# Attention beside a feed-forward chain: TensorE's order fixed in the first chunk, and the other chunks recorded as one spaced sequence

## The chip, the core and the metric

The kernel runs on one core of a Trainium2 chip. The metric is device time in microseconds (us), and lower is better. The engines are named as in the profile: PE is the matmul engine (PEld its weight loads, which overlap the matmuls), DVE the vector engine, ACT the scalar engine, POOL the GpSimd engine, and SP the engine whose queue issues the DMAs.

## What is computed

Attention with a hash mask, and then two feed-forward layers over its output. There are 2 batches, 8 heads, 768 positions and 64 features per head; the feed-forward layers are 512 wide with 2048 hidden features.

```python
q_bits = (np.einsum('bhsd,dk->bhsk', q, proj) > 0)          # 6 bits; the same for k
mask = q_bucket[:, :, :, None] == k_bucket[:, :, None, :]   # same 6 bits
scores = np.where(mask, scale * q @ k.T, -1e9)
scores = scores - np.max(scores, axis=-1, keepdims=True)
attn = np.exp(scores)
attn = attn / (np.sum(attn, axis=-1, keepdims=True) + 1e-09)
x = attn @ v                                                # 1536 tokens x 512
x = np.maximum(x @ w_in, 0.0) ** 2 @ w_out                  # layer 0
h = x @ w_in2
out = (np.maximum(h, 0.0) + alpha * np.minimum(h, 0.0)) @ w_out2   # layer 1
```

## The kernel before

The 1536 tokens are cut into 4 chunks of 384 (half a batch each). Attention of a chunk works on 4 pairs of heads (`Pair`). A pair has 6 score tiles (2 heads x 3 blocks of 128 queries). For each of them `scores` issues 4 matmuls of 128x384 on PE into one `s` tile, DVE takes the row maximum (`low`, line 389), ACT the exponential with its sums (`sm`, line 392), and `p_t` then turns the tile with 6 transposes on PE (line 407), three to an `m` tile, which DVE or ACT copies to `pt`. When a pair's six tiles are turned, `recip` makes the reciprocal of the sums (a small transpose into `rin`, line 437, and a trip through memory to spread it), `av` issues the 12 products with the values (line 423; the trace has 24 records for them), and `finish` scales the result and splits it into `xh` and `xl`. Before a pair's scores its queries, and in chunks 0 and 2 its keys, have to be prepared (`prepare`: hash bits, line 235; codes, line 251; splits and copies).

A feed-forward layer runs over a chunk in 16 units, one for each 128 hidden features. A unit is 12 matmuls in `hidden` (lines 613 to 615) and 9 in `project` (lines 641, 642, 645) into the tile `acc`; the projection of a unit is recorded one unit late. Layer 0 of chunk 0 starts when attention of chunk 0 has ended, and attention of chunks 1, 2 and 3 is recorded beside layer 0 of chunks 0, 1 and 2: `Background` holds a list of attention steps, and at 80 points of a chunk (`step()`) it runs as many of them as a straight line through its marks says. In the same place weights are changed from 64-bit floats to 32 bits (`to_f32`, three DVE operations and one ACT each).

The `s` tiles come from `s_tile`: in the first chunk two of them alternate, but beside the feed-forward chain there is only one, since `acc` then belongs to `project`. Codes of the keys use it too. `m` tiles rotate over three buffers in the first chunk and over two later.

What PE does next is not the recorded order alone: a scheduler goes through the recorded instructions by priority (recorded earlier is higher) and takes a later one where its own model of time says that the earlier one is not ready. `keep_in_program_order` and `issue_after` bind it. Every engine then runs its list strictly in that order, so where an instruction has to wait on the chip, all behind it on that engine wait as well.

Attention of one chunk is recorded by `attention(c, lag)`, which begins with the preparation of its first pair and ends by turning, multiplying and finishing its last one:

```python
    steps, marks = [], [(0.0, 0)]
    for c in range(1, NCH):
        steps += attention(c, 1)
        marks.append((c - 1 + LEAD, len(steps)))
    following = Background(steps, marks)
```

Of the kernel before, what the change touches and what calls it, by code (L numbers as in the profile page):

```python
# [1 line left out]

# [20 lines left out]

EVICT = ("aavaav", "avavav", "vvavva", "vvavva")

LEAD = 0.8


@with_exitstack
def kernel(  # L30
# [20 lines left out]
    nc = tc.nc  # L51
# [3 lines left out]
    P = 128  # L55
    T = S // 2
    NTB = T // P
    NKB = S // P
    NPAIR = H // 2
    NCH = NT // T  # L60
# [35 lines left out]
    def s_tile():  # L96

        state["s"] += 1
        if not state["moe"] and state["s"] % 2 == 0:
            return ps_a.tile([P, 3, 512], F32, tag="acc", name="acc")  # L100
        return ps_s.tile([P, 2, 512], F32, tag="s", name="s")

    def m_tile():

        state["m"] += 1
        if not state["moe"] and state["m"] % 3 == 0:
            return ps_h.tile([P, 512], F32, tag="h", name="h")
        return ps_m.tile([P, 512], F32, tag="m", name="m")
# [8 lines left out]
    def f32(ap):  # L117
        return ap.bitcast(F32)
# [4 lines left out]
    ident = const.tile([P, P], F32, name="ident")  # L123
# [47 lines left out]
    raw = {}  # L171
    keys = {}
    keyed = {}
    scored = {}

    def load_pair(c, j):

        b, s0 = c // 2, (c % 2) * T
        h0 = 2 * j
        kr = None  # L180
        if c % 2 == 0:
            kr = p2.tile([P, 2, S], F32, tag="kr", name="kr")
            nc.sync.dma_start(out=kr[:, 1], in_=kT[b, h0:h0 + 2].rearrange("h d s -> (h d) s"))
            if c == 0 and j == 0:
                nc.sync.dma_start(
                    out=proj_sb, in_=proj[:, 0:P].rearrange("p (h n) -> p h n", h=2)[:, :, 0:GR // 2]
                )
        qn = p2.tile([P, T], F32, tag="qn", name="qn")
        nc.sync.dma_start(out=qn, in_=qT[b, h0:h0 + 2, :, s0:s0 + T].rearrange("h d s -> (h d) s"))
        if c % 2 == 0:  # L190
            keys[b, j] = [kr, None, None]
            if c == 0 and j == 0:
                load_values(b, j)
                nc.sync.dma_start(out=ident, in_=eye)
                nc.sync.dma_start(out=alpha_sb, in_=alpha)
        raw[c, j] = qn

    def load_values(b, j):
        vr = p4.tile([P, NKB, 2 * D], F32, tag="vr", name="vr")
        keys[b, j][-1] = vr  # L200
        return nc.sync.dma_start(out=vr, in_=v[b, j])

    class Pair:
# [174 lines left out]
        def scores(self, h, t):  # L378
            ps = s_tile()
            qs = slice(t * P, (t + 1) * P)  # L380
            for a in range(2):
                ks = slice(a * HALF, (a + 1) * HALF)
                for i in range(2):
                    nc.tensor.matmul(  # L384
                        ps[:, a, 0:HALF], self.q[:, h, i, qs], self.k[:, h, i, ks], start=i == 0, stop=i == 1
                    )

            low = p4.tile([P, 1], F32, tag="low", name="low")
            low_ins = nc.vector.tensor_reduce(low, ps[:, 0:2, 0:HALF], AX.XY, ALU.max, negate=True)  # L389
            sm = sm3.tile([P, S], F32, tag="sm", name="sm")  # L390
            i = h * NTB + t
            sm_ins = nc.scalar.activation(  # L392
                sm.rearrange("p (a n) -> p a n", a=2), ps[:, 0:2, 0:HALF], AF.Exp, bias=low,
                accum_out=self.sums[:, i:i + 1],
            )
            scored[self.c, self.j, i] = (low_ins, sm_ins)
            self.p[h, t] = sm

        def p_t(self, h, t, a):
            if t == 0 and a == 0:  # L400
                self.pt[h] = p2.tile([P, NTB, NKB, P], F32, tag="pt", name="pt")
            pp = self.p[h, t]
            ps = m_tile()
            n = NKB // 2
            for i in range(n):
                b = a * n + i
                nc.tensor.transpose(ps[:, i * P:(i + 1) * P], pp[:, b * P:(b + 1) * P], ident)  # L407
            src = ps[:, 0:n * P].rearrange("p (b n) -> p b n", b=n)
            dst = self.pt[h][:, t, a * n:(a + 1) * n, :]
            if EVICT[self.c][2 * t + a] == "a":  # L410
                nc.scalar.activation(dst, src, AF.Copy)
            else:
                nc.vector.tensor_copy(dst, src)

        def av(self, part):

            if part == 0:
                self.o = m_tile()
            n = NKB // 3
            for b in range(part * n, (part + 1) * n):  # L420
                for h in range(2):
                    r = slice(h * D, (h + 1) * D)
                    nc.tensor.matmul(  # L423
                        self.o[r, 0:T], self.vr[:, b, r], self.pt[h][:, :, b, :],
                        start=(b == 0), stop=(b == NKB - 1),
                    )
            if part == 2:
                self.u = p1.tile([P, T], F32, tag="u", name="u")
                nc.scalar.activation(self.u, self.o[:, 0:T], AF.Copy)
# [17 lines left out]
        def finish(self):  # L447
            xh, xl = xT.get(self.c) or new_x(self.c)
            x = self.u
            nc.vector.tensor_tensor(x, x, self.rb, ALU.mult)  # L450
            nc.scalar.activation(xh[:, self.j, :], x, AF.Copy)
            nc.gpsimd.tensor_tensor(xl[:, self.j, :], x, f32(xh[:, self.j, :]), ALU.subtract)  # L452

    def new_x(key):
        xT[key] = (
            m2.tile([P, KDM, T], F32R, tag="xh", name="xh"),
            m2.tile([P, KDM, T], F32R, tag="xl", name="xl"),
        )
        return xT[key]

    def attention(c, lag):

        def begin():
            if (c, 0) not in raw:
                load_pair(c, 0)

        pairs = [Pair(c, j) for j in range(NPAIR)]
        steps = [begin] + pairs[0].prepare()
        late = []
        ended = []  # L470

        def tail():
            pr, h, t = late.pop(0)
            for a in range(2):
                steps.append(lambda a=a: pr.p_t(h, t, a))
            if t == NTB - 1 and h == 1:
                steps.append(pr.recip)
                for part in range(3):
                    steps.append(lambda part=part: pr.av(part))
                ended.append(pr)  # L480

        for j, pr in enumerate(pairs):
            nxt = pairs[j + 1].prepare() if j + 1 < NPAIR else []
            for u in range(2 * NTB):
                h, t = divmod(u, NTB)
                steps.append(lambda pr=pr, h=h, t=t: pr.scores(h, t))
                late.append((pr, h, t))
                for _ in range(2 if c == 0 else 1):
                    if nxt:
                        steps.append(nxt.pop(0))  # L490
                if ended and u == 3:
                    steps.append(ended.pop().finish)
                if len(late) > lag:
                    tail()
        while late:
            tail()
        while ended:
            steps.append(ended.pop(0).finish)
        return steps


    class Background:
# [52 lines left out]
    def keep(u):  # L555

        kept[u] = state["res"].tile([P, DM], F32, name="w%d_%d_%d" % u)
        nc.sync.dma_start(out=kept[u], in_=w_d[u])
# [169 lines left out]
    for step in attention(0, 2):  # L728
        step()
# [10 lines left out]
    state["moe"] = True  # L740


    steps, marks = [], [(0.0, 0)]
    for c in range(1, NCH):
        steps += attention(c, 1)
        marks.append((c - 1 + LEAD, len(steps)))
    following = Background(steps, marks)
    steps = []
    for f in range(KFF):
        for o in range(2):  # L750
# [19 lines left out]
    steps = [lambda f=f, o=o: keep((1, f, o)) for f in range(KFF) for o in range(2)]  # L770
    conversion = Background(steps, [(0.25, 0), (1.3, len(steps))])
    for n in range(NCH + 1):
        steps = second_x(n) if n < NCH else []
# [76 lines left out]
```

## Time and profile before

| | |
|---|---|
| median of 3 runs | 845.5 us (843.67 to 845.7) |
| the profiled execution's own time | 845.31 us |
| its span, from the first to the last instruction | 843.5 us |
| PE busy | 800.3 us, 95% of the span |
| PEld, DVE, ACT, POOL busy | 77%, 60%, 56%, 43% |
| mean granted clock of PE | 0.994 |

Busy shares are means over stages that differ: attention of chunk 0 alone (to about 82 us), layer 0 of chunks 0, 1 and 2 with attention beside it (to about 493 us), and then feed-forward alone. Matmuls overlap in the records, so a busy PE can still be issuing at less than its pace.

### The profile page before, as it was taken

What the parts mean: (1) busy time and instruction counts of PE and PEld (TensorE: products, weight loads), DVE (VectorE), ACT (ScalarE), POOL (GpSimd) and SP (SyncE); (2) the same over time, 40 slices, a digit from 0 to 9 for tenths busy, and PEclk for the clock granted to TensorE, in tenths of its full rate; (3) what the DMA queues carried; (4) which work ended last, traced back from release to release, by engine and by line L of the source; (5) the groups of instructions that cost most, each with busy time, mean ns of one, the idle gap of its engine ahead of it and who ended that gap; (6) DMA issues with size and microseconds to landing.
All of it is one profiled execution on the core that took longest, in us unless ns stands there. A gap on an engine that the chain in (4) does not pass through costs nothing.

```text
span 843.5 us, 12642 instructions
## 1 busy us (share of the span) xinstructions
PE 800.3 (95%) x4384; PEld 649.7 (77%) x4384; DVE 507.3 (60%) x822; ACT 473.7 (56%) x926; POOL 363.9 (43%) x321
## 2 busy tenths in 40 slices
PE   6999899999999999999999999999999999999997
PEld 4665777776768767586787789989989998998996
DVE  7678799887447658688897531224435445444442
ACT  5677677776557557475565556654434444444342
POOL 1002233233446646533333345555555555555553
PEclk9999899999999999999999999999999999999999
DMA  6757678775867687587765589600101011001001
GB/s 181 200 154 244 200 245 254 249 241 179 243 194 212 201 231 254 177 280 248 210 203 184 166 295 329 204 38 1 38 1 37 1 39 38 1 1 37 1 1 38
DMA packets 54863, 127.61 MB, mean 151 GB/s; under 512 B 7216, under 2 KB 11600, under 8 KB 54800
## 3 DMA queue, kind: packets, MB, share of 16 engines
q1 hardware_dynamic: 54800, 126.81, 48.1%
q8 instruction: 34, 0.56, 0.3%
q14 instruction: 29, 0.24, 0.1%
HBM read 82.93 MB, written 23.12 MB: 126 GB/s over the span
## 4 chain that ended last, share of the span: by engine, by line
PE 46%; DVE 3%; issue 2%; POOL 1%; ACT 1%; DMA 0%; POOLq 0%; DVEq 0%; ACTq 0%
PE acc L645 7%; PE acc L641 7%; PE acc L642 7%; PE m L615 4%; PE m L613 4%; PE m L614 4%; PE h L613 3%; PE h L615 3%; PE h L614 3%; PE m L423 2%; PE s L384 1%; POOL gl L631 1%; DVE low L389 1%; PE m L407 1%; PE s L717 1%
## 5 line engine op out<-in xcount | busy, mean ns | idle before, releaser
L631 POOL TENSOR_TENSOR gl<-g,gh 128x384 fp32r<-128x384 f32 x128 | 135.8, 1061 | 256.1 <-ACT gh L630 122.7
L641 PE MATMUL acc<-wh,gh 128*128 128x512 f32 x384 | 158.1, 412 | 0.0
L642 PE MATMUL acc<-wl,gh 128*128 128x512 f32 x384 | 151.7, 395 | 0.0
L566 POOL TENSOR_TENSOR wl<-wf,wh 128x512 fp32r<-128x512 f32 x80 | 108.6, 1362 | 99.4 <-ACT wh L565 80.2
L565 ACT ACTIVATE wh<-w 128x512 fp32r<-128x512 f32 x128 | 80.5, 629 | 80.7 <-PE m L614 45.7
L645 PE MATMUL acc<-wh,gl 128*128 128x512 f32 x384 | 116.1, 398 | 2.3 <-POOL gl L631 2.3
L565 ACT ACTIVATE wh<-wf 128x512 fp32r<-128x512 f32 x128 | 79.7, 628 | 58.5 <-PE h L614 23.6
L613 PE MATMUL h<-xh,wh 128*128 128x384 f32 x296 | 106.0, 358 | 1.5 <-ACT r L621 0.8
L389 DVE TENSOR_REDUCE low<-s 128x1 f32<-128x768 f32 x84 | 80.0, 952 | 41.8 <-PE s L384 41.6
L615 PE MATMUL h<-xh,wl 128*128 128x384 f32 x296 | 101.9, 344 | 1.2 <-POOL wl L566 1.2
L614 PE MATMUL h<-xl,wh 128*128 128x384 f32 x296 | 101.2, 342 | 0.6 <-POOL xl L452 0.6
L392 ACT ACTIVATE sm<-s,low 128x768 f32<-128x768 f32 x84 | 75.7, 901 | 33.8 <-DVE low L389 33.4
L384 PE MATMUL s<-k,q 128*128 128x384 f32 x336 | 80.7, 361 | 13.7 <-ACT sm L392 13.6
L645 PEld LDWEIGHTS acc<-wh,gl 128*128 128x128 f32 x384 | 71.7, 188 | 22.5 <-POOL gl L631 5.5
L566 POOL TENSOR_TENSOR wl<-w,wh 128x512 fp32r<-128x512 f32 x64 | 83.1, 1298 | 6.0 <-ACT wh L565 6.0
L641 PEld LDWEIGHTS acc<-wh,gh 128*128 128x128 f32 x384 | 72.3, 188 | 15.8 <-issue 4.8
L407 PE MATMUL m<-ident,sm 128*128 128x128 f32 x531 | 81.8, 275 | 2.2 <-ACT sm L392 1.0
L384 PEld LDWEIGHTS s<-k,q 128*128 128x128 f32 x336 | 58.1, 193 | 31.8 <-ACT sm L392 25.2
L630 ACT ACTIVATE gh<-g 128x384 fp32r<-128x384 f32 x64 | 33.5, 524 | 81.8 <-DVE g L629 81.8
L642 PEld LDWEIGHTS acc<-wl,gh 128*128 128x128 f32 x384 | 72.4, 189 | 8.8
L628 DVE TENSOR_SCALAR r<-m,alpha_sb 128x384 f32<-128x384 f32 x43 | 26.6, 618 | 86.9 <-PE m L615 86.7
L407 PEld LDWEIGHTS m<-ident,sm 128*128 128x128 f32 x531 | 64.9, 141 | 14.0 <-ACT sm L392 2.4
(117 smaller groups left out, 1432.8 us busy)
## 6 DMA issues: line engine op xcount, KB each, us to landing
wf<-w SPq DMA_DIRECT2D x96, 256.0 KB, 3.7
wbits<-in_w_in_dram SPq DMA_DIRECT2D x32, 512.0 KB, 4.0
wbits<-in_w_out_dram SPq DMA_DIRECT2D x32, 512.0 KB, 3.9
q<-q SPq DMA_DIRECT2D x48, 192.0 KB, 3.8
w<-wf SPq DMA_DIRECT2D x32, 256.0 KB, 2.3
w<-we SPq DMA_DIRECT2D x32, 256.0 KB, 2.3
w<-w SPq DMA_DIRECT2D x32, 256.0 KB, 4.5
k<-kh SPq DMA_DIRECT2D x14, 384.0 KB, 5.2
```

Source lines behind the costliest of these rows:

```text
L384: nc.tensor.matmul(ps[:, a, 0:HALF], self.q[:, h, i, qs], self.k[:, h, i, ks], start=i == 0, stop=i == 1)
L389: low_ins = nc.vector.tensor_reduce(low, ps[:, 0:2, 0:HALF], AX.XY, ALU.max, negate=True)
L407: nc.tensor.transpose(ps[:, i * P:(i + 1) * P], pp[:, b * P:(b + 1) * P], ident)
L565: nc.scalar.activation(hi, w, AF.Copy)
L566: engine.tensor_tensor(lo, w, f32(hi), ALU.subtract)
L613: nc.tensor.matmul(hp, wih[:, ks], xh[:, kk, :], start=first, stop=False)
L614: nc.tensor.matmul(hp, wih[:, ks], xl[:, kk, :], start=False, stop=False)
L615: nc.tensor.matmul(hp, wil[:, ks], xh[:, kk, :], start=False, stop=last)
L631: nc.gpsimd.tensor_tensor(gl, g, f32(gh), ALU.subtract)
L641: nc.tensor.matmul(acc[:, t, :], gh[:, blocks[t]], woh, start=first, stop=False)
L642: nc.tensor.matmul(acc[:, t, :], gh[:, blocks[t]], wol, start=False, stop=False)
L645: nc.tensor.matmul(acc[:, t, :], gl[:, blocks[t]], woh, start=False, stop=last)
```

## The change

Two things change. In the first chunk, the matmuls of scores, the transposes of `p_t` and the products of `av` are chained: each is bound behind the one recorded before it (`in_turn`). The other PE work (hash bits, codes, the transpose in `recip`) still goes where the scheduler puts it.

```diff
-LEAD = 0.8
+LEAD = 0.88
...
+    placed = []
+
+    def in_turn(c, product):
+
+
+        if c:
+            return product()
+        with tc.issue_after(placed.pop().ins) if placed else nullcontext():
+            ins = product()
+        placed.append(ins)
+        return ins
...
-                    nc.tensor.matmul(
+                    in_turn(self.c, lambda: nc.tensor.matmul(
...
-                nc.tensor.transpose(ps[:, i * P:(i + 1) * P], pp[:, b * P:(b + 1) * P], ident)
+                in_turn(
+                    self.c, lambda: nc.tensor.transpose(ps[:, i * P:(i + 1) * P], pp[:, b * P:(b + 1) * P], ident)
+                )
```

And attention of chunks 1 to 3 is recorded by a new function as one sequence of 12 pairs, without an end and a beginning at each chunk: the next pair is prepared during the scores of this one also across chunks, the values of a pair are multiplied between the first scores of the next, and `finish` comes with the last score tile of the next pair (with its fourth, where a chunk ends). The marks say that attention of chunk c + 1 is recorded by 0.88 of feed-forward chunk c, where 0.8 stood.

```diff
+    def attention_beside():
+
+
+        pairs = [Pair(c, j) for c in range(1, NCH) for j in range(NPAIR)]
+        steps, ends = [], []
...
+        def finish(pr):
+            steps.append(pr.finish)
+            if pr.j == NPAIR - 1:
+                ends.append(len(steps))
+
+        steps += [begin] + pairs[0].prepare()
+        last = 2 * NTB - 1
+        for n, pr in enumerate(pairs):
+            old = pairs[n - 1] if n else None
+            prep = pairs[n + 1].prepare() if n + 1 < len(pairs) else []
+            for u in range(2 * NTB):
+                steps.append(lambda pr=pr, u=u: pr.scores(*divmod(u, NTB)))
+                if prep and u != 1:
+                    steps.append(prep.pop(0))
+                if u == 0 and old:
+                    turn(old, last)
+                    steps.append(old.recip)
+                    values(old, 0)
+                if u == 1 and old:
+                    values(old, 1)
+                    values(old, 2)
+                if u:
+                    turn(pr, u - 1)
+                if u == 4 and prep:
+                    steps.append(prep.pop(0))
+                if u == (3 if old and old.j == NPAIR - 1 else last) and old:
+                    finish(old)
...
-    steps, marks = [], [(0.0, 0)]
-    for c in range(1, NCH):
-        steps += attention(c, 1)
-        marks.append((c - 1 + LEAD, len(steps)))
-    following = Background(steps, marks)
+    steps, ends = attention_beside()
+    following = Background(steps, [(0.0, 0)] + [(c + LEAD, n) for c, n in enumerate(ends)])
```

Line numbers of the changed kernel are higher: 384 became 395 (scores), 407 became 419 (transposes), 423 became 436 (values), 437 became 450, and the feed-forward lines moved by 65.

Three places on PE follow, as the scheduler left them. The first is in the first chunk, where the third pair hands over to the fourth. Before, PE has this row of work:

```order
L407 MATMUL m<-ident,sm 128x128 x3
L384 MATMUL s<-k,q 128x384 x3
L423 MATMUL h<-pt,vr 64x384 x3
L437 MATMUL m<-ident,rin 6x128
L423 MATMUL h<-pt,vr 64x384 x9
L384 MATMUL s<-k,q 128x384
L407 MATMUL m<-ident,sm 128x128 x6
```

Of the change, at the same place:

```order
L419 MATMUL m<-ident,sm 128x128 x3
L436 MATMUL h<-pt,vr 64x384 x5
L450 MATMUL m<-ident,rin 6x128
L436 MATMUL h<-pt,vr 64x384 x7
L395 MATMUL s<-k,q 128x384 x4
L419 MATMUL m<-ident,sm 128x128 x6
```

Three of the four score matmuls stood ahead of the values and the fourth behind them; now all four stand behind.

The second place is the end of attention of chunk 2, near the end of layer 0 of chunk 1 (the numbers behind wh and wl are buffers of a unit's weights). Before, PE has:

```order
L645 MATMUL acc<-wh_3855,gl 128x512 x2
L407 MATMUL m<-ident,sm 128x128 x6
L645 MATMUL acc<-wh_3855,gl 128x512
L613 MATMUL h<-xh,wh_3945 128x384
L437 MATMUL m<-ident,rin 6x128
L614 MATMUL h<-xl,wh_3945 128x384
L423 MATMUL m<-pt,vr 64x384 x8
L615 MATMUL h<-xh,wl_3946 128x384
L613 MATMUL h<-xh,wh_3945 128x384
L614 MATMUL h<-xl,wh_3945 128x384
L615 MATMUL h<-xh,wl_3946 128x384
L423 MATMUL m<-pt,vr 64x384 x4
```

Of the change, where the same pair ends:

```order
L450 MATMUL m<-ident,rin 6x128
L706 MATMUL acc<-wh_3904,gh 128x512
L707 MATMUL acc<-wl_3905,gh 128x512
L436 MATMUL m<-pt,vr 64x384 x4
L395 MATMUL s<-k,q 128x384 x4
L706 MATMUL acc<-wh_3904,gh 128x512
L707 MATMUL acc<-wl_3905,gh 128x512
L710 MATMUL acc<-wh_3904,gl 128x512 x3
L436 MATMUL m<-pt,vr 64x384 x4
L678 MATMUL h<-xh,wh_3988 128x384
L679 MATMUL h<-xl,wh_3988 128x384
L680 MATMUL h<-xh,wl_3989 128x384
```

Before, no scores stand between the last transposes and the end of the values; now scores of the next pair stand among the values, and the feed-forward matmuls lie between rin and the first of them.

The third place is the start of layer 0 of chunk 1, where attention of chunk 2 begins. Before, PE has this in the first unit:

```order
L384 MATMUL s<-k,q 128x384 x4
L407 MATMUL m<-ident,sm 128x128 x6
L641 MATMUL acc<-wh_2783,gh 128x512
L642 MATMUL acc<-wl_2784,gh 128x512
L641 MATMUL acc<-wh_2783,gh 128x512
L642 MATMUL acc<-wl_2784,gh 128x512
L641 MATMUL acc<-wh_2783,gh 128x512
L642 MATMUL acc<-wl_2784,gh 128x512
L645 MATMUL acc<-wh_2783,gl 128x512
L384 MATMUL s<-k,q 128x384 x4
L407 MATMUL m<-ident,sm 128x128 x6
```

Of the change, in the third unit there:

```order
L395 MATMUL s<-k,q 128x384 x4
L678 MATMUL h<-xh,wh_2899 128x384
L679 MATMUL h<-xl,wh_2899 128x384
L680 MATMUL h<-xh,wl_2900 128x384
L678 MATMUL h<-xh,wh_2899 128x384
L679 MATMUL h<-xl,wh_2899 128x384
L680 MATMUL h<-xh,wl_2900 128x384
L419 MATMUL m<-ident,sm 128x128 x3
L706 MATMUL acc<-wh_2903,gh 128x512
L707 MATMUL acc<-wl_2904,gh 128x512
L419 MATMUL m<-ident,sm 128x128 x3
```

Where two score tiles followed each other with six transposes and seven matmuls between them, the next user of the `s` tile now comes after more work, and the transposes stand in two blocks of three.

## Rows read from the trace of the kernel before

**Rows 1.** Windows by stage: length; then busy time and count by engine, clock, DMA.
```profile
82.27:223.15 140.88, 132.13 (x763) 101.84 (x761) 115.56 (x184) 97.83 (x199) 45.91 (x38) 0.98 0.73 231
223.15:370.46 147.31, 139.70 (x806) 104.97 (x805) 98.55 (x144) 88.33 (x178) 80.51 (x68) 0.99 0.73 220
370.46:493.08 122.62, 116.89 (x660) 91.28 (x657) 91.31 (x147) 70.23 (x143) 42.57 (x35) 1.00 0.66 212
...
563.37:837.92 274.55, 273.17 (x1380) 245.27 (x1379) 120.89 (x206) 114.17 (x201) 144.85 (x127) 1.00 0.05 18
```

**Rows 2.** The same view: five feed-forward units with no attention beside them.
```profile
505.28:526.22 20.94, 20.94 (x107) 18.97 (x106) 3.46 (x5) 12.91 (x25) 11.31 (x10) 1.00 0.96 325
```

**Rows 3.** Timeline of PE (start, length): a score tile, six transposes, then feed-forward.
```profile
97.62 0.86 PE L384 MATMUL s<-k,q 128*128 128x384 f32 x4
98.32 0.82 PE L407 MATMUL m<-ident,sm 128*128 128x128 f32 x6
98.89 0.42 PE L613 MATMUL h<-xh,wh 128*128 128x384 f32 x1
99.15 0.33 PE L614 MATMUL h<-xl,wh 128*128 128x384 f32 x1
99.32 0.34 PE L615 MATMUL h<-xh,wl 128*128 128x384 f32 x1
```

**Rows 4.** Timeline of PE: the products with the values of one pair.
```profile
78.25 4.09 PE L423 MATMUL m<-pt,vr 128*64 128x384 f32 x24 [0.35 <-ACT pt L411]
```

**Rows 5.** Windows of line 384 (score matmuls) alone: PE busy and count.
```profile
98.89:161.60 62.71, 13.09 (x56) 9.21 (x56) 1.00 0.78 247
376.38:426.74 50.36, 7.57 (x33) 5.42 (x32) 1.00 0.75 233
...
304.41:376.38 71.97, 11.73 (x52) 8.85 (x52) 0.98 0.72 232
```

**Rows 6.** Windows of line 423 (values) alone, the same stretches.
```profile
98.89:161.60 62.71, 8.40 (x48) 3.18 (x48) 1.00 0.78 247
376.38:426.74 50.36, 8.62 (x48) 3.09 (x48) 1.00 0.75 233
...
304.41:376.38 71.97, 11.34 (x48) 3.70 (x48) 0.98 0.72 232
```

**Rows 7.** Waits of PE, 82.27 to 493.08 us: total, times, longest.
```profile
PE s L384 <- ACT sm L392: 11.0, 18, 1.4
PE m L437 <- DVE pt L413: 2.0, 2, 1.8
PE m L251 <- DVE bits L239: 1.9, 3, 0.7
```

**Rows 8.** Costliest groups of the page: the maximum and the exponential.
```profile
L389 DVE TENSOR_REDUCE low<-s 128x1 f32<-128x768 f32 x84 | 80.0, 952 | 41.8 <-PE s L384 41.6
...
L392 ACT ACTIVATE sm<-s,low 128x768 f32<-128x768 f32 x84 | 75.7, 901 | 33.8 <-DVE low L389 33.4
```

**Rows 9.** Waits of PE in the first chunk, 4.29 to 82.27 us.
```profile
PE s L384 <- ACT sm L392: 2.6, 4, 1.6
PE acc L384 <- ACT sm L392: 0.9, 2, 0.5
```

**Rows 10.** Timeline of PE in the first chunk: third pair to fourth.
```profile
63.34 0.80 PE L384 MATMUL s<-k,q 128*128 128x384 f32 x3 [0.37 <-ACT sm L392]
64.06 1.50 PE L423 MATMUL h<-pt,vr 128*64 128x384 f32 x6
...
65.70 3.44 PE L423 MATMUL h<-pt,vr 128*64 128x384 f32 x18
69.07 0.44 PE L384 MATMUL s<-k,q 128*128 128x384 f32 x1
```

**Rows 11.** Windows: a busy stretch of DVE, and a stretch at a lower clock.
```profile
100.00:180.00 80.00, 76.44 (x449) 58.44 (x448) 75.06 (x120) 62.00 (x128) 24.84 (x21) 1.00 0.77 249
340.00:346.00 6.00, 5.02 (x19) 2.04 (x20) 2.98 (x8) 1.03 (x2) 1.50 (x2) 0.72 0.69 209
```

More of the change, by code (lines that the diff above doesn't have):

```diff
@@ L1 @@
-from contextlib import ExitStack
+from contextlib import ExitStack, nullcontext
 import concourse.bass as bass
@@ L383, in scores @@
                 for i in range(2):
-                    nc.tensor.matmul(
+                    in_turn(self.c, lambda: nc.tensor.matmul(
                         ps[:, a, 0:HALF], self.q[:, h, i, qs], self.k[:, h, i, ks], start=i == 0, stop=i == 1
-                    )
+                    ))
             low = p4.tile([P, 1], F32, tag="low", name="low")
@@ L422, in av @@
                     r = slice(h * D, (h + 1) * D)
-                    nc.tensor.matmul(
+                    in_turn(self.c, lambda: nc.tensor.matmul(
                         self.o[r, 0:T], self.vr[:, b, r], self.pt[h][:, :, b, :],
                         start=(b == 0), stop=(b == NKB - 1),
-                    )
+                    ))
             if part == 2:
@@ L499, in attention, with begin, turn, values @@
         return steps
+    def attention_beside():
+        pairs = [Pair(c, j) for c in range(1, NCH) for j in range(NPAIR)]
+        steps, ends = [], []
+        def begin():
+            if (1, 0) not in raw:
+                load_pair(1, 0)
+        def turn(pr, u):
+            for a in range(2):
+                steps.append(lambda a=a: pr.p_t(*divmod(u, NTB), a))
+        def values(pr, part):
+            steps.append(lambda: pr.av(part))
+        def finish(pr):
[24 more added lines that the diff above has]
+                    finish(old)
+            assert not prep
+        turn(pr, last)
+        steps.append(pr.recip)
+        for part in range(3):
+            values(pr, part)
+        finish(pr)
+        return steps, ends
     class Background:
```

## The prediction

> **What bounds the kernel now.** I read the shares first: PE is busy 95% of the span, so the time is PE's, and the question is how much of a busy PE is pace and how much is standing still. The windows by stage come next. In layer 1 PE issues 1380 records in 274.55 us, and five units without attention take 20.94 us, 4.19 us each [rows 1, 2]. That is PE at its pace: 12 matmuls at 0.174 us and 9 at 0.233 us. The reader should see in the same rows that PEld has 245.27 of 274.55 us there (89%), but 101.84 of 140.88 (72%), 104.97 of 147.31 (71%) and 91.28 of 122.62 (74%) in the three stages with attention beside layer 0, although PE itself counts as 94 to 95% busy in them.
>
> The Trainium skill says why these shares differ (Perfetto Trace Analysis, Identifying the Most-Contended Engine): a matmul's busy time is a poor measure of how far PE is from its limit, the share of weight loads a better one. This trace agrees, 95% against 72%. By the busy share at most 22 us would be open in these stages; by the count that follows it is about 69.
>
> The count: beside feed-forward, a score tile costs 0.70 us of PE and its six transposes 0.57 (starts at 97.62, 98.32 and 98.89), and a pair's products with the values 4.09 us [rows 3, 4]. The three stages hold 48 units, 72 score tiles and 12 pairs: 48 x 4.19 + 72 x 1.27 + 12 x 4.09 = 201 + 91 + 49 = 341.6 us. They last 410.8 us [rows 1]. So 69 us are lost to waits, to hash bits and codes, to changes between kinds of matmul and to a lowered clock.
>
> Where it is lost is seen by stretches between unit starts. From 98.89 to 161.60 us lie 7 units, 14 score tiles (56 matmuls) and two pairs' products: 29.3 + 17.8 + 8.2 = 55.3 of 62.7 us, 1.06 us lost per unit [rows 5, 6]. From 376.38 to 426.74 lie 6 units, 8 tiles and two products: 43.5 of 50.4, 1.14 per unit. In both the attention comes in an even stream. From 304.41 to 376.38, where attention of chunk 2 ends and that of chunk 3 begins, lie 8 units, 13 tiles and two products: 58.2 of 72.0, 1.7 per unit. There PE granted only 0.72 of its clock between 340 and 346 us [rows 11], which at its two levels of 1.2 and 2.4 GHz means 3.4 of 6 us at the lower one, 1.7 us of pace lost. The list of waits names the same: 18 waits of scores for the exponential, 11.0 us; two of the small transpose in recip, 2.0; three of codes for bits, 1.9 [rows 7]. A score tile can't be refilled until DVE's maximum (952 ns) and ACT's exponential (901 ns) have read it [rows 8]; with the end of the last score matmul and two handovers I estimate from these rows that 2.5 us must lie between two uses of the one s tile.
>
> **The change, part by part.** No operation is added or removed: every matmul, copy and DMA is issued as often as before. Only the order moves, with these effects.
>
> *The sequence beside layer 0.* First, what the program order shows, priced by rows 2 to 4: before, 32 of 75 pairs of neighbouring uses of the s tile have less than 2.5 us of PE work between them (11 in layer 0 of chunk 0, 18 of chunk 1, 3 of chunk 2); after, 19 of 75 (14, 4, 1). The third place shown is one of the 18. At 11.0 us for the 32 [rows 7], 13 fewer are worth 4.5 us. Second, the two chunk ends inside the stream vanish: the second place shows scores among the values and six feed-forward matmuls' room where PE had only values. I take both together by the even pace. The two first units (82.27 to 98.89 us, until the last pair of chunk 0 is finished) lose 8.4 us: 16.6 less 2 x 4.19, less two score tiles and one set of transposes, plus 2.1 for the one projection that isn't yet due there. These stay. The other 46 units lose 69 - 8.4 = 60.8 us, 1.32 each. At the even pace of about 1.12 it would be 51.5, so 9.3 us less.
>
> Against this stands a cost. After a block of transposes, the next feed-forward matmul comes after 0.26 us where the one behind it comes after 0.17 (98.89, 99.15, 99.32) [rows 3]: 0.09 us for each such block. The program has 131 blocks of transposes and 34 of values beside layer 0 where it had 113 and 28, so 24 x 0.09 = 2.2 us. The even stretches hold their share of blocks already, but in the old, longer form; I take half, 1.1 us.
>
> Third, PE work moves between stages: layer 0 of chunk 0 has 30 score tiles beside it instead of 25, chunk 1 has 25 instead of 28, and chunk 2 17 instead of 19. PE pays the same wherever they stand. DVE does not: it is busy 115.56 of 140.88 us in chunk 0 and 98.55 of 147.31 in chunk 1 [rows 1], and five maxima at 0.95 are 4.8 us [rows 8]; the copies and preparation that go with them have no row of their own here, so between nothing and as much again. DVE then has 120 to 125 us in a stage that I expect to last 145: 83 to 86%, under the 75.06 of 80 (94%) that it already ran from 100 to 180 us [rows 11], a stretch that contains most of the first even one. So I add nothing for it.
>
> Fourth, the lead. With 0.88 attention of a chunk ends about one unit later. In the program order the last products for chunk 3 stand in the 15th of the 16 units, so one full unit (4.19 us) and the last one with its two projections (6.3 us) lie between them and the first use. After the products come one copy, one multiply, one split on ACT and one on POOL. From 82.27 us this tail cost PE most of the 8.4 us, with nothing to cover it; here 10 us cover it. I cost it at nothing, and at 3 us if the trip of the reciprocals through memory is late.
>
> The sum for this part: 9.3 - 1.1 = 8.2, about 8 us gained, with bounds of 3 (the score waits alone, 4.5, less the blocks' 2.2) and 19 (below).
>
> *The first chunk.* The first place shows what the chain does: the score tile that was split around the values comes behind them as one. On the chip, three score matmuls started at 63.34 after a wait of 0.37 us, the values at 64.06 and the fourth score matmul at 69.07 [rows 10]. The tile was complete only behind the values in both orders, so the maximum starts no earlier by the order; what can be saved is the wait, 0.37 us, three times, since the values then lie over the exponential. At the start of the chunk, where scores of two tiles were mixed, one tile comes out whole sooner. All waits of scores in this chunk are 2.6 + 0.9 = 3.5 us [rows 9]. Bounds: a gain of all of it, and a loss of the same size, if the fixed order makes PE stand at a product whose copy is late where the scheduler had put scores. I take a gain of 1 us, nearer to the three waits that the rows show.
>
> The sum: 845.3 us of the profiled execution (span 843.5 and 1.8 around it, close to the median of 845.5) less 8 less 1 gives about 836 us.
>
> **The rivals.** *The waits all but vanish.* If the spaced stream lets every score tile be free in time, the 11.0 us of scores, the 2.0 of recip, the 1.9 of bits and the 1.7 of the lower clock go, 16.6 us, and with the first chunk's 3.5 less 1.1 for blocks it is 845.3 - 19 = 826 us. For it: 4 and 1 short distances are left in the last two stages. Against it: 14 in the first, which are more than before.
>
> *The waits only move.* One s tile holds scores and codes alike, and the number of tiles is the same; the scheduler sets PE's order by its own model, as before, so each tile may wait as long as it did, elsewhere. Then the gain is the chunk ends' half of 9.3 at most, and the blocks cost 2.2: 843 to 846, about 845 us. The Trainium skill has the rule that speaks for it (Perfetto Trace Analysis, Optimization Strategy): a gap that repeats on the engine that should be full can mean too few buffers, and an order doesn't add one. The 18 waits at one line, 0.6 us each, look like that. Against it are the even stretches, where the same single tile loses a third less per unit.
>
> *DVE becomes the bound beside chunk 0 (slower).* The maximum, the copies out of m and three of the operations that change weights all queue on DVE in order; if the five more tiles put it at its limit, late copies hold transposes and late weights hold hidden. The price: layer 0 of chunk 0 loses 2.0 instead of 1.12 us per unit over 14 units, 12.3 us, and 836 becomes 848. It decides from 1.8 per unit on. For it: 94% from 100 to 180 us. Against it: that stretch lost only about 1.1 per unit with DVE so full, and the last 20 us of the stage had room.
>
> **How the numbers follow.** The forecast near 836 (830 to 842) has a chance of 0.52; the waits vanish (822 to 830) 0.2; they only move 0.17; DVE bounds 0.09; 0.02 is left for still lower times. This kernel's runs tell 0.3% from no change, 843.0 to 848.0 us. Faster: 0.52 + 0.2 + 0.02, and a little of the third case, 0.76. Same: 0.15. Slower: 0.09. The range 823 to 846 holds the forecast's case, nearly all of the second and third, and leaves out DVE's case and the lowest times; I keep the third case whole in it since it is the one that would turn the sign.
>
> **What would show it.** Right: the three stages last about 402 us instead of 410.8, the first of them longer (about 148) and the second shorter (about 131); the waits of scores for the exponential fall from 11.0 to 6 or 7 us, with none at the two chunk ends; no lower clock near the end of attention of chunk 2; the first chunk ends within 1 us or so of 82.3. Wrong: the first stage over 155 us with DVE above 93%; or the score waits still at 11; or waits of hidden for xh, xl at a chunk's start, which would be the lead; or a first chunk that moves by more than 3.5 us, which would be the chain.

## The result, and the profile after

The changed kernel takes 837.8 us (median of 5 runs, 835.25 to 839.74), the kernel before 845.7 beside it; the ratio is 0.9915, with a 95% interval of 0.989 to 0.994. It is faster by 0.85%, nearly three times what a measurement of this kernel can tell. The profiled execution took 839.74 us, with a span of 838.0.

The windows by stage, which answer to [rows 1] and the first of [rows 11]; the stages begin and end at the first hidden matmul of a chunk:

```profile
83.18:233.13 149.95, 141.31 (x844) 108.82 (x842) 126.58 (x203) 107.00 (x220) 47.27 (x38) 0.98 0.77 233
233.13:368.35 135.22, 128.53 (x753) 98.80 (x754) 96.01 (x138) 81.75 (x165) 77.54 (x66) 1.00 0.75 232
368.35:486.00 117.65, 114.48 (x629) 87.97 (x628) 86.75 (x133) 67.84 (x135) 41.49 (x35) 1.00 0.62 196
556.70:831.28 274.58, 273.19 (x1380) 245.25 (x1379) 120.74 (x206) 114.21 (x201) 144.54 (x127) 1.00 0.05 18
100.00:180.00 80.00, 77.10 (x456) 58.08 (x455) 73.19 (x117) 60.22 (x124) 24.86 (x19) 1.00 0.76 237
```

The first stage is 149.95 us (140.88 before), the second 135.22 (147.31), the third 117.65 (122.62): together 402.8 in place of 410.8 us, 8.0 less. Layer 1 is the same to 0.03 us. DVE works 126.6 us in the first stage, 84% of it, and 73.2 of 80 us between 100 and 180 us, where it had 75.1. The two profiled executions lie 5.6 us apart, not 8.0, because three places elsewhere are later: the first chunk ends at 83.18 and not at 82.27 us, chunk 3 of layer 0 takes 0.4 us more, and the last output lands 1.1 us later behind the last matmul.

The waits of PE in the three stages (total, times, longest), which answer to [rows 7]:

```profile
PE s L395 <- ACT sm L403: 7.9, 10, 1.6
PE h L678 <- ACT xh L464: 2.7, 1, 2.7
PE m L419 <- ACT q L328: 2.4, 3, 1.4
PE s L395 <- DVE kr L286: 1.4, 3, 0.5
PE m L419 <- DVE bits L250: 1.1, 1, 1.1
```

Scores wait 7.9 us in 10 places for the exponential (11.0 in 18), and another 1.4 for DVE's reading of the codes, which share the tile. The wait of hidden for xh is the start of layer 0, 2.7 us here and 0.7 before; no such wait stands at the start of chunks 1 to 3, so no cost of the lead is seen. The fewer waits lie in the third stage. In the second, which gains most, they are the same, first before and then with the change:

```profile
PE s L384 <- ACT sm L392: 3.0, 6, 1.1
PE s L395 <- ACT sm L403: 3.2, 4, 1.6
```

The granted clock is 1.00 in the second and third stage; the low stretch near the end of attention of chunk 2 [rows 11] is gone.

The score matmuls alone (count in brackets), which answer to [rows 5] by stage:

```profile
83.18:233.13 149.95, 28.52 (x120) 20.76 (x120) 0.98 0.77 233
233.13:368.35 135.22, 22.69 (x100) 17.09 (x100) 1.00 0.75 232
368.35:486.00 117.65, 15.22 (x68) 11.76 (x68) 1.00 0.62 196
```

That is 30, 25 and 17 tiles (4 matmuls each), as the program order said. And in the first chunk, the place of [rows 10]:

```profile
63.92 2.15 PE L436 MATMUL h<-pt,vr 128*64 128x384 f32 x10 [0.28 <-ACT pt L424]
...
66.21 2.79 PE L436 MATMUL h<-pt,vr 128*64 128x384 f32 x14
68.93 0.96 PE L395 MATMUL s<-k,q 128*128 128x384 f32 x4
```

The values start at 63.92 (64.06 before) and the whole score tile at 68.93, behind them.

### The profile page after: what moved, and what is told of

The parts are those of the page before. It is cut to its first block, busy times and chain, and to the rows that moved or that the text cites. A ratio compares the mean times of both kernels' runs of the same rounds, so it can differ in the third digit from the quotient of the medians.

```text
span 838.0 us, 12642 instructions
## 1 busy us (share of the span) xinstructions
PE 796.1 (95%) x4384; PEld 648.7 (77%) x4384; DVE 512.9 (61%) x822; ACT 474.5 (57%) x926; POOL 359.9 (43%) x321
## 4 chain that ended last, share of the span: by engine, by line
PE 66%; DVE 13%; DMA 8%; ACT 5%; issue 4%; POOL 1%; SPq 1%; POOLq 0%; DVEq 0%; ACTq 0%
PE acc L710 8%; PE acc L706 8%; PE acc L707 8%; PE s L395 5%; PE h L678 5%; PE h L679 5%; PE h L680 4%; PE m L680 4%; PE m L678 4%; PE m L679 4%; PE m L436 4%; PE m L419 4%; DMA w<-we 2%; DVE wsg L607 2%; DVE low L400 2%
## 5 line engine op out<-in xcount | busy, mean ns | idle before, releaser
L696 POOL TENSOR_TENSOR gl<-g,gh 128x384 fp32r<-128x384 f32 x128 | 134.0, 1047 | 263.7 <-ACT gh L695 123.0
L706 PE MATMUL acc<-wh,gh 128*128 128x512 f32 x384 | 160.4, 418 | 0.0
L710 PE MATMUL acc<-wh,gl 128*128 128x512 f32 x384 | 113.8, 396 | 1.8 <-POOL gl L696 1.8
L419 PE MATMUL m<-ident,sm 128*128 128x128 f32 x531 | 86.6, 277 | 6.3 <-ACT q L328 2.4
```

The source lines that it names most:

```text
L419: self.c, lambda: nc.tensor.transpose(ps[:, i * P:(i + 1) * P], pp[:, b * P:(b + 1) * P], ident)
L696: nc.gpsimd.tensor_tensor(gl, g, f32(gh), ALU.subtract)
L706: nc.tensor.matmul(acc[:, t, :], gh[:, blocks[t]], woh, start=first, stop=False)
L710: nc.tensor.matmul(acc[:, t, :], gl[:, blocks[t]], woh, start=False, stop=last)
```

## The experiments

Each kernel was timed beside the kernel before; the ratio is to that kernel, with its 95% interval in brackets.

**The two parts apart.** In the first kernel `attention_beside` is replaced by the old loop over `attention(c, 1)` with `LEAD = 0.8`. In the second the chain is off:

```diff
-        if c:
+        if c >= 0:
             return product()
```

> The chain in the first chunk alone; attention beside layer 0 as before, with lead 0.8. Theory 1 (the sequence beside layer 0 makes the whole gain, the chain is worth nothing or costs): layer 0 of chunk 0 starts at 83.2 us as in the changed kernel (82.3 before), because the chain makes PE stand about 2 us at 21 us for a transpose; 845 to 847 us, ratio 1.000 +- 0.003. Theory 2 (the chain carries a part of the gain, by what it hands to the units behind it): 841 to 844 us, ratio 0.995 to 0.998.

> The sequence beside layer 0 with lead 0.88 alone; first chunk as before. Theory 1: 836 to 838 us, ratio 0.988 to 0.992, the three stages of layer 0 together about 402 to 403 us as in the changed kernel, first chunk until 82.3 us: a little better than the changed kernel. Theory 2: 839 to 842 us, ratio 0.993 to 0.996.

The chain alone: 1.0002 (0.9991 to 1.0012). The sequence alone: 0.9915 (0.9903 to 0.9928), 836.7 us at 844.1 for before. The sequence makes the whole gain, and the chain is worth nothing. With the chain, PE waits for other things in the first chunk:

```profile
PE h L419 <- ACT q L336: 2.1, 1, 2.1
PE m L419 <- ACT pt L424: 1.0, 2, 0.9
```

The 2.1 us are transposes that stand, by program order, where PE had other work. After this wait the clock is at its lower level for a while (the column behind the engines is the granted clock):

```profile
20.00:25.00 5.00, 4.14 (x19) 4.05 (x20) 2.00 (x3) 4.02 (x8) 0.00 (x0) 0.66 0.90 218
```

The same wait, of 2.2 us, and the same low stretch are in the changed kernel. Against them stand about 3 us less of score waits in the chunk (0.5 us where [rows 9] have 3.5).

Beside layer 0 the kernel with the chain alone has the old recording, so it also shows what a second profile of that recording gives. Its stages are 138.7, 145.9 and 121.6 us, 406.2 together, where the profile before has 410.8, and its clock between 340 and 346 us is full:

```profile
340.00:346.00 6.00, 6.00 (x34) 2.94 (x34) 2.78 (x5) 1.18 (x2) 0.60 (x1) 1.00 0.67 224
```

So single stages of two profiles can differ by 1 to 2 us without any change, and the missing low stretch of [rows 11] is not shown to be an effect of the new order. The windows of the sequence alone add up to 401.7 us:

```profile
82.77:230.66 147.89, 140.63 (x847) 108.44 (x846) 125.00 (x202) 106.29 (x219) 48.12 (x38) 0.99 0.77 236
230.66:368.10 137.44, 129.44 (x751) 98.46 (x749) 88.61 (x139) 81.34 (x165) 76.90 (x66) 1.00 0.75 227
368.10:484.51 116.41, 114.55 (x630) 87.90 (x628) 81.16 (x133) 67.58 (x135) 41.37 (x35) 1.00 0.63 203
```

**The lead, and the spread of the values.** On the sequence alone, in one kernel `LEAD = 0.8`, in the other the three steps of values are recorded at once:

```diff
                     steps.append(old.recip)
-                    values(old, 0)
-                if u == 1 and old:
-                    values(old, 1)
-                    values(old, 2)
+                    for part in range(3):
+                        values(old, part)
```

> The sequence alone, with the old lead 0.8. Theory 1 with the stream across chunk ends as the cause: the gain stays, 836 to 840 us, although layer 0 of chunk 0 gets denser (over 152 us in place of 150). Rival (the later lead, which thins the stream beside chunks 0, is the cause): 843 to 847 us, near the kernel before.

> The sequence alone with lead 0.88, but a pair's three steps of values recorded one behind the other after the transposes, as before, and not between the first two score tiles of the next pair. If the gain comes from the chunk ends, this is within 1 us of the sequence alone (836 to 839 us). If it comes from spreading the values so that score tiles are spaced, the waits of scores for the exponential rise from 8 to 10 or 11 us and it takes 840 to 843 us.

0.9933 (0.9917 to 0.995) and 0.9932 (0.992 to 0.9945), 837.5 and 837.7 us. Neither is told from the sequence alone. With the values together, scores waited 8.5 us (5.5 in the sequence alone) and the longest pauses between score tiles were 11 to 12 us (at most 9 in the sequence alone), and the median moved by 0.9 us only. So neither the lead nor the spread of the values carries the gain; the intervals leave room for an effect of up to 3 us of either.

**The chunk change: preparation, or draining?** The sequence does two things there. In one kernel the old order is kept (values together, each chunk turned, multiplied and finished before the next one's scores, lead 0.8), and only the preparation crosses the chunk's end:

```diff
+        for n, pr in enumerate(pairs):
+            nxt = pairs[n + 1].prepare() if n + 1 < len(pairs) else []
...
+            if pr.j == NPAIR - 1:
+                while late:
+                    tail()
+                while ended:
+                    steps.append(ended.pop(0).finish)
```

In the other it is the sequence without that:

```diff
-            prep = pairs[n + 1].prepare() if n + 1 < len(pairs) else []
+            prep = pairs[n + 1].prepare() if n + 1 < len(pairs) and pr.j < NPAIR - 1 else []
+            if n and pr.j == 0:
+                steps += pr.prepare()
```

> Attention beside layer 0 as before (lag 1, values together, lead 0.8, each chunk drained and finished before the next one's scores), but the first pair of chunks 2 and 3 is prepared during the scores of the last pair of the chunk ahead. If the missing preparation at a chunk's start is the main part of what the sequence gains: 4 to 6 us faster than before, ratio 0.993 to 0.995. If it is the draining at a chunk's end: 0 to 2 us, ratio 0.998 to 1.000.

> The sequence alone (lead 0.88), but the first pair of chunks 2 and 3 is prepared in one go at its chunk's start, as before; the last pair of the chunk ahead still ends among the new pair's scores. If the preparation is the main part: most of the gain is lost, 841 to 844 us, ratio 0.997 to 1.000. If the draining is: 837 to 839 us, ratio 0.992 to 0.995.

The preparation ahead alone: 0.988 (0.9853 to 0.9908), 834.1 us at 844.9. That is the whole gain of the change with one of its ingredients, and twice what I expected of it. The sequence without it: 0.9946 (0.9927 to 0.9964), 840.4 us, a bit more than half the gain: not draining closes some of the pause by itself (16.4 us without a score tile ahead of chunk 2, where the kernel before has 27.3). The two do not add up; they are two ways to the same end.

**DVE beside chunk 0, and the blocks of transposes.** On the sequence alone, `EVICT[1] = "aaaaaa"` in place of `"avavav"`; and `turn` records both halves of a tile as one step.

> The sequence alone, and in chunk 1 all copies of turned tiles are made by ACT in place of half of them by DVE: 24 copies of 0.55 us, 13 us of DVE work less beside chunk 0 and 12 us of ACT work more. If DVE is the bound beside chunk 0: layer 0 of chunk 0 becomes 4 to 8 us shorter than the sequence's 147.9, 829 to 833 us. If the bound there is PE's own work and the chain of a score tile, which ends on ACT: within 2 us of the sequence, or 1 to 3 us slower.

> The sequence alone, with the two sets of three transposes of a score tile recorded as one step. The program has 124 blocks of transposes in place of 171. If each block costs the 0.09 us that the trace before shows: 47 x 0.09 = 4 us faster than the sequence alone, 832 to 834 us, ratio 0.986 to 0.989. If spacing matters more than blocks (the transposes then take both m tiles at once and PE waits for copies): the same or up to 2 us slower than the sequence, ratio 0.991 to 0.994.

With the copies on ACT: 0.9874 (0.9853 to 0.9895), 834.1 us, about 0.4% better than the sequence alone. But not where DVE was relieved:

```profile
81.40:231.99 150.59, 143.67 (x843) 109.17 (x842) 113.67 (x178) 113.43 (x243) 45.21 (x38) 0.98 0.77 229
231.99:363.04 131.05, 127.69 (x753) 98.74 (x754) 93.41 (x139) 82.33 (x165) 76.90 (x66) 1.00 0.77 239
363.04:479.59 116.55, 114.84 (x629) 87.87 (x628) 84.72 (x134) 67.74 (x135) 42.10 (x35) 1.00 0.64 204
```

DVE fell from 125.0 to 113.7 us in the first stage, and the stage did not get shorter (150.6 and 147.9 us); the second did (131.0 and 137.4). DVE alone was not the bound beside chunk 0; ACT got 7.1 us more to do there, so the run does not separate the two. The transposes together: 0.9937 (0.9921 to 0.9953). With 47 blocks fewer no time was saved, where 4 us were expected; what their other spacing cost is not separated from it.

**Which chunk change?** On the kernel with the preparation ahead: `EVICT[1] = "aaaaaa"` with it, then the preparation ahead for chunk 2 alone and for chunk 3 alone, then lead 0.88:

```diff
+            cold = n + 1 < len(pairs) and pairs[n + 1].j == 0 and pairs[n + 1].c != 2
+            if n and pr.j == 0 and pr.c != 2:
+                steps += pr.prepare()
-            nxt = pairs[n + 1].prepare() if n + 1 < len(pairs) else []
+            nxt = pairs[n + 1].prepare() if n + 1 < len(pairs) and not cold else []
```

> The preparation ahead over the chunk end (old order otherwise, lead 0.8) and chunk 1's copies of turned tiles all on ACT. If what the copies give (about 3 us on the sequence) adds to what the preparation gives (10.8): 830 to 833 us at 845 for the kernel before, ratio 0.982 to 0.986, the best so far. If DVE's relief only did there what the preparation does here: 0.987 to 0.990.

> Preparation ahead for the first pair of chunk 2 alone (keys and queries); chunk 3's is prepared at its start as before. Theory: the gain comes from the two stretches without a score tile at the chunk changes (28 us before chunk 2 and 21 us before chunk 3 in the trace before), each about half: 4 to 7 us, ratio 0.992 to 0.995. Rival (chunk 2's start alone matters, since its preparation has the keys and the five steps): 9 to 11 us, ratio 0.987 to 0.989.

> Preparation ahead for the first pair of chunk 3 alone (queries, two steps). Theory: 4 to 7 us, ratio 0.992 to 0.995, and with chunk 2's alone it adds up to the 10.8 us of both. Rival: 0 to 2 us, ratio 0.998 to 1.000.

> Preparation ahead at both chunk changes as in the earlier run, with lead 0.88 in place of 0.8. If the lead is worth nothing, as with the sequence: ratio 0.986 to 0.990. If a thinner stream beside chunk 0 helps: 0.982 to 0.986. If the later end of attention costs (waits of hidden for xh and xl at a chunk's start): 0.990 to 0.994.

Chunk 2 alone: 0.9847 (0.9823 to 0.9871), 830.2 us at 844.2, the fastest median of all and more than even the rival said (its interval overlaps that of the preparation at both changes, so leaving chunk 3 out is not shown to help). Chunk 3 alone: 0.9989 (0.9973 to 1.0004). My theory of two equal halves fell; the rival holds: the start of chunk 2 is the place. With the copies on ACT 0.9865 (0.9849 to 0.9882), with lead 0.88 0.9891 (0.9873 to 0.9909): neither is told from the preparation ahead alone.

The windows of the score matmuls alone show it. Before, by stage and then in the two pauses at the chunk changes:

```profile
82.27:223.15 140.88, 23.54 (x100) 17.36 (x100) 0.98 0.73 231
223.15:370.46 147.31, 26.32 (x113) 18.85 (x112) 0.99 0.73 220
370.46:493.08 122.62, 17.46 (x76) 12.88 (x76) 1.00 0.66 212
195.00:222.40 27.40, 0.19 (x2) 0.17 (x1) 1.00 0.71 205
335.00:355.00 20.00, 0.15 (x1) 0.07 (x1) 0.91 0.58 182
```

For 27.4 us at the start of attention of chunk 2 PE has no score tile but the edges of two, and for 20.0 us at the start of that of chunk 3. With chunk 2 prepared ahead, the same five windows (the last two are again the pauses):

```profile
82.89:228.28 145.39, 27.83 (x120) 20.19 (x120) 0.99 0.76 232
228.28:357.71 129.43, 21.01 (x92) 15.66 (x92) 1.00 0.81 243
357.71:481.67 123.96, 17.15 (x76) 13.09 (x76) 0.99 0.63 204
194.10:205.50 11.40, 0.15 (x1) 0.14 (x1) 1.00 0.77 251
324.00:342.60 18.60, 0.04 (x1) 0.00 (x0) 1.00 0.84 260
```

The first pause is 11.4 us, and five tiles moved out of the second stage (112 matmuls become 92) into the first. The pause before chunk 3 is still 18.6 us; with the preparation at both changes it is 14.1 us, and the time is no shorter. With chunk 3 prepared ahead alone, and the pause before chunk 2:

```profile
81.24:221.64 140.40, 23.68 (x100) 17.27 (x100) 0.98 0.74 232
221.64:370.65 149.01, 28.16 (x120) 20.41 (x120) 1.00 0.72 218
370.65:487.91 117.26, 15.51 (x68) 11.73 (x68) 1.00 0.68 219
194.00:220.20 26.20, 0.11 (x1) 0.17 (x1) 1.00 0.69 206
```

That pause is as long as before, the second stage has 30 tiles, and 149.0 us. And with the chain alone, which has the old recording:

```profile
83.11:221.80 138.69, 23.76 (x100) 17.32 (x100) 0.99 0.73 233
221.80:367.70 145.90, 26.31 (x113) 18.83 (x112) 1.00 0.73 221
367.70:489.34 121.64, 17.45 (x76) 12.86 (x76) 1.00 0.66 214
```

The waits of scores for the exponential over the three stages, from the list of waits of the kernel with the preparation ahead at every chunk change:

```profile
PE s L384 <- ACT sm L392: 7.2, 9, 2.1
```

And the same of the kernel with chunk 2 alone:

```profile
PE s L384 <- ACT sm L392: 8.2, 10, 2.0
```

Both are about what the changed kernel has, 7.9 us, though they are 3 and 6 us faster by their ratios. The fewest of all twelve but one, 4.3 us, are in the sequence without the preparation ahead, which gains least of the sequences.

The loss by stage, with the prices of the prediction (4.19 us a unit, 1.27 a tile, 4.09 a pair), from the windows above. Each stage has 16 units and 4 pairs, 83.4 us, so the first stage of the changed kernel lost 149.95 - 83.4 - 30 x 1.27 = 28.5 us:

```
                       stage 1          stage 2          stage 3
                    tiles    lost    tiles    lost    tiles    lost
before                25     25.7      28     28.3      19     15.1
chain alone           25     23.5      28     26.9      19     14.1
changed kernel        30     28.5      25     20.1      17     12.7
chunk 2 ahead         30     23.9      23     16.8      19     16.4
chunk 3 ahead         25     25.3      30     27.5      17     12.3
```

The first two rows are the same recording, so 1 to 2 us in a place of this table mean nothing. (The profiled execution of chunk 2 ahead took 834.1 us at a median of 830.2, that of chunk 3 ahead 840.6 at 842.2.) What stands clear of that is the second stage: it loses 7 to 12 us less where the pause before chunk 2 is closed. The first stage takes five more tiles there, at a loss between 2 us less and 5 us more. Counted the same way, all kernels here divide by that pause: where it is 26 to 27 us (before, the chain alone, chunk 3 ahead) the second stage loses 27 to 28 us and the ratio is 0.999 to 1.000; in the others, with at most 16.4 us, that stage loses 16 to 24 us, and the ratio is 0.985 to 0.995. Among those the pause does not order the times: the sequence alone has no stretch over 9 us without a score tile, and the old order with the preparation ahead, with a pause of 11 us there, is faster.

## Why the prediction was right, and where it was not

The number (836 for 837.8) and its main term hold: the three stages gained 8.0 us where 8 were forecast. That they agree so closely is in part luck. The 8 was 9.3 less a cost of 1.1 that the runs do not show, and the shares came out otherwise: the stages last 150, 135 and 118 us where 148, 131 and, as the rest of 402, 123 were expected. The steps behind the number fared unequally.

**The chunk ends.** Right as the place: the second stage carries the gain, 12.1 us shorter with three tiles fewer. (The low clock went too, but it is also absent in a profile of the old recording.) But I had put two equal chunk changes into an even pace. The runs showed that one does the work: the start of chunk 2, whose first pair had to have its keys and queries split, coded and moved while no score tile could run. Why the second stage then loses less is seen (the table) but not taken apart. The edit closes the pause and also moves five tiles into the first stage, and no run separates the two; with 30 tiles in place of 28 the second stage lost no more. That the pause before chunk 3 is harmless was tried only as far as the runs went, since preparing it ahead alone shortened it from 20.0 to 15.1 us and no further.

**The spacing of score tiles.** Half of the argument (4.5 us at 11.0 us for 32 short distances), and wrong as a cause. The counts came out as the program order said, and the waits fell to 7.9 us, near the 6 or 7 forecast. But the price was not in the trace: before, the second stage, with 18 of the 32 short distances, has 3.0 us of these waits, and the third, with 3, has 5.4. With the change the second stage waits 3.2 us and still loses 8 us less, so its gain is not in them. And the kernels with the old spacing and chunk 2 prepared ahead wait as long (7.2 and 8.2 us) and are faster, and with the values together again the time hardly moved.

**The blocks.** The 1.1 us for more blocks is a cost that the kernel's time does not show: 47 blocks fewer brought nothing. The 0.09 us at each is real in the rows, but it was a price taken from a place, not from the path.

**The lead at nothing** and **DVE not the bound beside chunk 0**: right as far as a run each can tell. With DVE relieved the second stage is shorter, by a way that no run here separates.

**The start of layer 0.** "These stay" was not quite so. Hidden waits 0.7 us there for xh where neither the chain nor the sequence is in the kernel, and 1.6 to 2.7 us where one of them or both are, with either lead: a cost of 1 to 2 us that the sum had at nothing, and that was overlooked.

**The first chunk.** The gain of 1 us was mis-sized: it measured nothing, by the ratio of the chain alone. (The 0.9 us by which the chunk ends later in the profile tell nothing: in the profiles of kernels whose first chunk is unchanged it ends between 81.2 and 83.5 us.) I had named the loss (PE standing where the scheduler had put other work) and given it as a bound; the runs show it, 2.2 us in one wait with a stretch at the lower clock behind it, against 3 us less of score waits.

Of the rivals, none came: the waits did not vanish, did not merely move, and DVE was not seen as the bound. "The waits only move" was nearest to the truth in one thing: the score waits are not what the time hangs on.

## What to carry to other kernels

Where one stream of work is laid beside another, look first for the long pauses in it, and not for the short waits: a pause of 27 us shows in no list of waits, since the engine is busy with the other stream. Here the time came back in the stage behind it; that it is paid there because the displaced work is packed is a guess that no run shows. Count the instructions of one line in windows along the stage, and prepare the next piece before the last one ends. When a change has several ingredients, try each alone: here one step of preparation, ahead at one of two places, gave 1.5% where the whole rewrite gave 0.85%.

## What the runs showed that was not expected

A single wait on PE of about 2 us was followed by a stretch at the lower of the two clock levels, 1.2 GHz: the granted clock was 0.66 in the mean between 20 and 25 us with the chain, where the kernel before was granted 1.00 between 20 and 30 us. The wait alone does not decide it. Three kernels with the first chunk unchanged (copies on ACT, with and without the preparation ahead, and chunk 3 ahead) have a wait of 1.9 us at the same place; behind it the clock is at the lower level in one of them (copies on ACT with the preparation ahead) and full in the other two, of which the second line is one:

```profile
20.00:22.00 2.00, 2.00 (x10) 1.90 (x10) 0.96 (x1) 1.94 (x4) 0.00 (x0) 0.50 0.95 209
20.00:22.00 2.00, 1.53 (x11) 1.12 (x10) 1.42 (x2) 1.98 (x5) 0.00 (x0) 1.00 1.05 230
```

And a price read from neighbouring starts on PE (0.09 us behind each block of transposes) did not add up: 47 such blocks less did not shorten the kernel.
